# A linear-attention pair on one core: one key product is regrouped when it is saved, not when it is read

## The chip, the cores and the metric

The kernel runs on one core of one Trainium2 chip. The metric is the device time of one execution in microseconds (us). An execution that was profiled has, beside its time, a span: the stretch that the profile covers. The smallest difference that a measurement of this kernel tells from none is taken as 2%.

## The reference

Two linear-attention blocks, A and B, read the same input x (2048 rows of 640) with weights of their own, and a sigmoid gate mixes their outputs.

```python
qkv = (x @ wqkv)            # 640 -> 3 * 640, 32 heads of 20
phi = lambda t: jnp.where(t > 0, t + 1, jnp.exp(t)) + 1e-6
pq, pk = phi(q), phi(k)
kv  = einsum("bhsd,bhse->bhde", pk, v)
z   = einsum("bhsd->bhd", pk)
o   = einsum("bhqd,bhde->bhqe", pq, kv) / (einsum("bhqd,bhd->bhq", pq, z)[..., None] + 1e-6)
block(x) = o @ wo
g = sigmoid((x * gate_w).sum(-1))
out = g * block_A(x) + (1 - g) * block_B(x)
```

All tensors are bfloat16; sums are kept in float32.

## The kernel before, in words

The 2048 rows are 16 tiles of 128 rows. The work runs in stages whose order on TensorE (PE) is written out by hand in the string `MAIN`.

- **Keys.** For each tile and each block, five pairs of matmuls (lines 653 and 654, 512 and 128 or 129 columns, one pair for each 128 of the 640 inputs) make the keys of the tile in two PSUM banks. Column 640 of block B holds the gate sum of each row. `k_post` turns them into phi(k): ScalarE (ACT) reads PSUM and takes the exponential into `EK`, a part of `EKT` (line 699); VectorE (DVE) clamps it to at most 1 and adds 1e-6 (`kt`, line 702); then either ACT writes relu(k) into `PKS` (line 711 where both blocks of a tile take this way, line 726 otherwise) and DVE adds the two (`ka`, line 717 for both blocks, line 729 for one), or DVE does maximum and addition from PSUM in one instruction (`ks`, line 738). The list `KRS` says which tile and block takes which way. For block B, ACT also takes exp(-gate) into `GE` (line 690).
- **Regrouping.** The keys come out of the matmul with column d of 640 at place (m, g), g running fastest in steps of 5. `k_post` reads them as (g, m): `psg` is a view with a step of five float32 values in the inner loop.
- **Tiles 12 and 13.** `ks_unit(6)` makes the keys of these two tiles and both blocks by a scheme of seven half products in place of eight (tokens `K6.1` to `K6.7` in `MAIN`, line 809). Two half products are saved from PSUM to float32 buffers in SBUF, `s5` and `s2` (`save`, line 815, on ACT; the buffers `KQ` lie in `PQ0`, which the profile calls `PQ`). `comb` (line 820, DVE) later adds the other half: in step 3 PSUM plus `s2` back into PSUM, in step 7 PSUM plus `s5` into `s5`. So the keys of block B of tile 13 stand in SBUF and not in PSUM when `k_post` takes exponential, relu and gate from them. The weight sums for the scheme are four DVE instructions in `kw_sums` (line 767), the row sums five in `kx_sums` (line 787).
- **Sums over rows.** The tokens G0 to G4 multiply phi(k) with x (line 1156) in groups of eight matmuls, one for each pair of tiles. They too use the scheme of seven products: their factors are differences of phi(k) (`s_pair`, line 879) and of x (`t_all`, line 904), made on DVE. `G0.1`, `G3.1` and so on are the steps; a step numbered 1 or 2 leaves out the last pair of tiles, 14 and 15, which 8 and 9 add later.
- After this come the queries (lines 1035 and 1124), the small products with the value and output weights, the denominators (line 1410) and the output products (line 1546), which are stored by DMA.

**What sets the order.** PE follows the order in which the operations are created. ACT, DVE and the DMA queues get their order from a planner in the kernel (`Sched.run`) before anything is emitted: each operation has an estimated cost, PSUM banks are given to buffers when they are planned to be free, and for each engine the operation that can start first is taken, or, at equal start, the one created first. The planner takes an engine to be free again `LATE` nanoseconds before the end of the operation's cost:

```python
self.occ = max(40.0, cost - LATE.get(eng, 0.0))
LATE = {"ACT": 110.0, "DVE": 80.0}
def act_cost(n): return 190 + 0.833 * n
```

The cost doesn't depend on where an operation reads or with what step.

Of the kernel before, what the change touches and what calls it, by code (L numbers as in the profile page):

```python
# [6 lines left out]
ACT = mybir.ActivationFunctionType  # L7
ALU = mybir.AluOpType
# [3 lines left out]
D = 640  # L12
# [3 lines left out]
NC = 5  # L16
# [49 lines left out]
WPDVE = ("A1", "B0",)  # L66
QD = ("0.0A0", "0.0A1", "0.1B0", "0.1B1", "0.2A0", "0.2B0", "0.2B1", "0.3A0", "1.0B1",)
RD = ("A0", "A1", "A4", "B0",)
LATE = {"ACT": 110.0, "DVE": 80.0}


class Buf:
# [37 lines left out]
class Sched:  # L110
# [9 lines left out]
    def op(self, eng, fn, cost, ins=(), outs=(), after=(), prio=None, name="", dma=None):  # L120
        if eng == "ACT" and dma is None:
            after = list(after) + self.consts
        o = Op(eng, fn, cost, list(ins), list(outs), after, (self.base or len(self.ops)) if prio is None else prio, name, dma)
        self.ops.append(o)
        return o
# [184 lines left out]
def body(nc, A_x, A_wqkv, A_wo, B_x, B_wqkv, B_wo, gate_w, out, log=None):  # L310
# [25 lines left out]
    GE = sb("GE", [128, NT], f32)  # L336
# [40 lines left out]
    KQ = [PQ0f[:, 1296 * i : 1296 * i + 1296].bitcast(f32) for i in range(2)]  # L377
# [53 lines left out]
    op = sch.op  # L431

    def psw(b, w):
        if b.pool == "kq":
            return KQ[b.slot][:, 0:w]
        return PS[:, b.slot : b.slot + b.n, :].rearrange("p a b -> p (a b)")[:, 0:w]

    chain, loading = {}, [1]
# [18 lines left out]
    def act_cost(n):  # L457
        return 190 + 0.833 * n
# [209 lines left out]
    def k_post(t, units):  # L668

        n = len(units)  # L670
        ek, ek2 = Buf("ek", "ek", n, (0, 2, 4)), Buf("ek2")
        exps = []

        def ev(i):
            return EK[:, ek.slot + i, :]

        def evg(i):
            return ev(i).rearrange("p (g m) -> p g m", g=NC)

        def psg(ps):  # L680
            return psw(ps, D).rearrange("p (m g) -> p g m", g=NC)

        for i, (X, ps, relu) in enumerate(units):
            first = []
            if X == "B":
                b = Buf("ge")
                bge.append(b)
                op(
                    "ACT",
                    lambda e, ps=ps: e.activation(GE[:, t : t + 1], psw(ps, D + 1)[:, D : D + 1], ACT.Exp, scale=-1.0),  # L690
                    200.0,
                    ins=[ps],
                    outs=[b],
                    name="ge",
                )
                first = [b]
            b = Buf("ekx")
            exps.append(b)
            op("ACT", lambda e, i=i, ps=ps: e.activation(evg(i), psg(ps), ACT.Exp), act_cost(D), ins=[ps] + first, outs=[ek, b], name="ke")  # L699
        op(  # L700
            "DVE",
            lambda e: e.tensor_scalar(EK[:, ek.slot : ek.slot + n, :], EK[:, ek.slot : ek.slot + n, :], 1.0, EPS, op0=ALU.min, op1=ALU.add),  # L702
            dve4(n * D),
            ins=[ek],
            outs=[ek2],
            name="kt",
        )
        if n == 2 and units[0][2] and units[1][2]:
            rk = Buf("rk")
            for X, ps, relu in units:  # L710
                op("ACT", lambda e, X=X, ps=ps: e.activation(pkt(X, t), psg(ps), ACT.Relu), act_cost(D), ins=[ps], outs=[rk], name="kr")  # L711
            pk = Buf("pk%d" % t)
            bpk["A", t] = bpk["B", t] = pk

            def both(e):
                v = PKv[:, :, t % 2, t // 2, :]
                return e.tensor_tensor(out=v, in0=v, in1=EK[:, ek.slot : ek.slot + 2, :].rearrange("p x (g m) -> p (x g) m", g=NC), op=ALU.add)

            pk_last.append(op("DVE", both, dve2(2 * D), ins=[rk, ek, ek2], outs=[pk], name="ka"))
            pk_last.append(pk_last[-1])  # L720
            return
        for i, (X, ps, relu) in enumerate(units):
            pk = bpk[X, t] = Buf("pk%s%d" % (X, t))
            if relu:
                rk = Buf("rk")
                op("ACT", lambda e, X=X, ps=ps: e.activation(pkt(X, t), psg(ps), ACT.Relu), act_cost(D), ins=[ps], outs=[rk], name="kr")  # L726
                o = op(
                    "DVE",
                    lambda e, X=X, i=i: e.tensor_tensor(out=pkt(X, t), in0=pkt(X, t), in1=evg(i), op=ALU.add),
                    dve2(D),  # L730
                    ins=[rk, ek, ek2],
                    outs=[pk],
                    name="ka",
                )
            else:
                o = op(
                    "DVE",
                    lambda e, X=X, i=i, ps=ps: e.scalar_tensor_tensor(pkt(X, t), psg(ps), 0.0, evg(i), op0=ALU.max, op1=ALU.add),  # L738
                    dve1(D),
                    ins=[ps, ek, ek2],  # L740
                    outs=[pk],
                    name="ks",
                )
            pk_last.append(o)
# [29 lines left out]
    def kx_sums():  # L774
        t1, t2 = 256 * KU, 256 * KU + 128
        a11, a12, a21, a22 = [XT[:, c : c + 2, lo : lo + 128] for lo in (t1, t2) for c in (0, 2)]
        for k, in0, in1, need in (
# [13 lines left out]
                name="kx",  # L791
            )

    def ks_unit(j):
        px, py, pz = [Buf("k", "ps", 2, cover=(512, 129)) for _ in range(3)]
        py.need = (512, 128)
        s2, s5 = [Buf("kq", "kq") for _ in range(2)]
        d = {}
        t1, t2 = 2 * j, 2 * j + 1

        def xt(c, h):
            return XT[:, c, 256 * j + 128 * h : 256 * j + 128 * h + 128]

        def mm(ps, w, first, prs, ins, after=()):
            def fn(e):
                a = psw(ps, w)
                for i, (m, l) in enumerate(prs):
                    for lo, hi in ((0, 512), (512, w)):
                        r = e.matmul(a[:, lo:hi], l, m[:, lo:hi], start=(first and i == 0), stop=(i == len(prs) - 1), skip_group_check=not first)  # L809
                return r  # L810

            kpe[:] = [op("PE", fn, len(prs) * (mm_cost(512) + mm_cost(128)), ins=ins, outs=[ps], after=after, name="K%d" % j)]

        def save(dst, ps, w):
            return op("ACT", lambda e: e.activation(psw(dst, w), psw(ps, w), ACT.Copy), act_cost(w), ins=[ps], outs=[dst], name="ksv")

        def comb(ps, src, into_src):
            return op(
                "DVE",
                lambda e: e.tensor_tensor(out=psw(src if into_src else ps, D + 1), in0=psw(ps, D + 1), in1=psw(src, D + 1), op=ALU.add),  # L820
                dve1(D + 1),
                ins=[ps, src],
                outs=[src if into_src else ps],
                name="kcm",
            )

        bx = [bxt[t1], bxt[t2]]

        def step(n):
            if n == 1:  # L830
                mm(px, D + 1, True, [(WK["A"][:, c, :], xt(c, 0)) for c in range(2)], bx + [bwk["A", c] for c in range(2)] + [bwz])
                d[1] = op("ACT", lambda e: e.activation(psw(py, D), psw(px, D), ACT.Copy), act_cost(D), ins=[px], outs=[py], name="kfk")
            elif n == 2:
                mm(py, D, False, [(WK["A"][:, c, :], xt(c, 0)) for c in range(2, 5)], bx + [bwk["A", c] for c in range(2, 5)])
            elif n == 5:
                mm(pz, D + 1, True, [(KW[1][:, c, :], KX[1][:, c, :]) for c in range(2)] + [(WK["B"][:, 4, :], xt(4, 1))], bx + [bkw[1], bkx[1], bwk["B", 4], bgc])
                d[5] = save(s5, pz, D + 1)
            elif n == 6:
                mm(px, D + 1, False, [(KW[2][:, c, :], KX[2][:, c, :]) for c in range(2)], [bkw[2], bkx[2]], [d[1]])
                d[2] = save(s2, px, D + 1)  # L840
            elif n == 3:
                mm(pz, D + 1, False, [(WK["B"][:, 2 + c, :], KX[4][:, c, :]) for c in range(2)] + [(WK["B"][:, 4, :], KX[5])], [bkx[4], bkx[5], bgc] + [bwk["B", c] for c in range(2, 5)], [d[5]])
                comb(pz, s2, False)
                k_post(t1, [("A", py, "%dA" % t1 in KRS), ("B", pz, "%dB" % t1 in KRS)])
            elif n == 7:
                mm(px, D + 1, False, [(KW[3][:, c, :], KX[3][:, c, :]) for c in range(2)], [bkw[3], bkx[3]], [d[2]])
                d[7] = comb(px, s5, True)
            elif n == 4:
                mm(px, D, False, [(KW[4][:, c, :], xt(2 + c, 1)) for c in range(2)] + [(WK["A"][:, 4, :], xt(4, 1))], bx + [bkw[4], bwk["A", 4]], [d[7]])
                for X, ps in (("B", s5), ("A", px)):  # L850
                    k_post(t2, [(X, ps, "%d%s" % (t2, X) in KRS)])

        return step
# [874 lines left out]
```

## Time and profile before

| | |
|---|---|
| time, median of three runs | 176.8 us |
| the three runs | 176.8, 176.49, 1020.49 us |
| time of the profiled execution | 176.63 us |
| span of the profiled execution | 175.2 us |
| granted TensorE clock | 1.00 |
| PE busy | 172.1 us, 1331 matmuls |
| DVE busy | 140.3 us, 246 instructions |
| ACT busy | 116.2 us, 221 instructions |

The table is read from the head and part 1 of the profile. A row of a view gives the line of the kernel, the engine and operation, what is written and what is read, the shape, the count, and busy time with the mean of one. "PEld" is the weight load that goes ahead of each matmul. In the view in order of time, a row has start, duration and, in brackets, how long the engine stood idle before it and who ended that. Instructions of one engine overlap a little there: the next starts before the one before it has ended, so what one instruction takes of its engine is the distance to the next start.

### The profile page before, as it was taken

To read this page: it belongs to the slowest core of one execution; us is meant where nothing else is said; L and a number is where in the kernel's file an instruction comes from. 1 tells how busy PE (TensorE), PEld (TensorE's weight loads), DVE (VectorE), ACT (ScalarE), POOL (GpSimd) and SP (SyncE) were. 2 spreads that over 40 slices of the span, in tenths; PEclk is the share of its full clock that TensorE was granted. 3 is DMA by queue.
4 is the path that set the end of the run, shared out by engine and by line. 5 is a ranking of instruction groups with operands and counts; after the bars stand their busy time and mean duration, and the time that the engine had idled before them with its cause. 6 is when DMAs were issued, how large, how long until landed. Compare 5 with 4: busy or idle time off the path is not lost.

```text
span 175.2 us, 3364 instructions
## 1 busy us (share of the span) xinstructions
PE 172.1 (98%) x1331; PEld 107.6 (61%) x1331; DVE 140.3 (80%) x246; ACT 116.2 (66%) x221; POOL 4.9 (3%) x17
## 2 busy tenths in 40 slices
PE   9999999999999999999999999999999999999995
PEld 4555555555557776665666665655556667777773
DVE  2298996999989957668975798799999985999441
ACT  5377889998972232558695788848799874366132
POOL 2000000000000070000000000000000000000000
PEclk9999999999999999999999999999999999999999
DMA  6979999990000015310531703267671011451144
GB/s 191 315 127 126 236 354 365 357 190 4 4 0 0 0 37 101 74 38 0 136 99 37 224 4 75 49 168 210 226 186 40 0 41 28 96 185 41 37 147 153
DMA packets 33035, 20.59 MB, mean 118 GB/s; under 512 B 18260, under 2 KB 32892, under 8 KB 33020
## 3 DMA queue, kind: packets, MB, share of 16 engines
q1 hardware_dynamic: 32062, 19.76, 43.4%
q10 hardware_dynamic: 958, 0.63, 1.2%
q8 instruction: 10, 0.16, 0.4%
q14 instruction: 5, 0.04, 0.1%
HBM read 10.88 MB, written 4.26 MB: 86 GB/s over the span
## 4 chain that ended last, share of the span: by engine, by line
PE 94%; ACT 4%; issue 1%; DVE 0%; ACTq 0%
PE ps L1546 22%; PE ps L1156 20%; PE ps L653 16%; PE ps L1035 13%; PE ps L1124 10%; PE ps L654 4%; ACT EKT L699 3%; PE ps L809 3%; PE ps L580 1%; PE ps L1410 1%; PE ps L1336 1%; PE ps L1304 1%; ACT PKS L711 1%; PE ps L593 1%; ACT PKS L726 0%
## 5 line engine op out<-in xcount | busy, mean ns | idle before, releaser
L653 PE MATMUL ps<-WKW,XT 128*128 128x512 bf16 x140 | 39.5, 383 | 0.2 <-ACT GE L690 0.2
L654 PE MATMUL ps<-WKW,XT 128*128 128x128 bf16 (+1 forms) x140 | 30.9, 221 | 0.0
L699 ACT ACTIVATE EKT<-ps 128x640 bf16<-128x640 f32 x31 | 21.6, 711 | 5.3 <-PE ps L654 4.8
L653 PEld LDWEIGHTS ps<-WKW,XT 128*128 128x128 bf16 x140 | 13.8, 99 | 17.2 <-issue 0.7
L1156 PE MATMUL ps<-TX,PKS 128*128 128x321 bf16 (+1 forms) x160 | 24.1, 300 | 0.0
L1156 PEld LDWEIGHTS ps<-TX,PKS 128*128 128x128 bf16 x160 | 15.7, 98 | 7.4
L1156 PE MATMUL ps<-XN,PKS 128*128 128x321 bf16 (+1 forms) x120 | 18.7, 300 | 0.4 <-ACT PKS L711 0.3
L1156 PEld LDWEIGHTS ps<-XN,PKS 128*128 128x128 bf16 x120 | 11.5, 98 | 6.3 <-ACT PKS L711 1.1
L1184 ACT ACTIVATE EKT<-ps 128x321 f32<-128x321 f32 (+1 forms) x15 | 6.5, 438 | 11.1 <-PE ps L1156 8.9
L654 PEld LDWEIGHTS ps<-WKW,XT 128*128 128x128 bf16 x140 | 13.8, 99 | 0.0
L1065 ACT ACTIVATE EQ<-ps 128x512 bf16<-128x512 f32 x18 | 10.6, 599 | 3.8 <-DVE ps L1049 2.4
L879 DVE TENSOR_TENSOR PKS<-PKS 128x1280 bf16<-128x1280 bf16 (+2 forms) x20 | 12.8, 682 | 0.0
L702 DVE TENSOR_SCALAR EKT<-EKT 128x1280 bf16<-128x1280 bf16 (+1 forms) x19 | 8.3, 436 | 4.4 <-ACT EKT L699 4.2
L1189 DVE TENSOR_TENSOR WKW<-ps,EKT 128x320 bf16<-128x320 f32 x15 | 7.3, 486 | 5.2 <-PE ps L1156 5.0
L711 ACT ACTIVATE PKS<-ps 128x640 bf16<-128x640 f32 x16 | 11.4, 711 | 0.0
L1135 ACT ACTIVATE EQ<-ps 128x1024 bf16<-128x1024 f32 x8 | 8.2, 1029 | 4.4 <-PE ps L1124 3.4
L1035 PE MATMUL ps<-XT,WQA 128*128 128x512 bf16 x36 | 10.4, 379 | 0.0
L1124 PE MATMUL ps<-XT,WQA 128*128 128x512 bf16 x40 | 9.2, 381 | 0.0
L1124 PE MATMUL ps<-XT,WQB 128*128 128x512 bf16 x40 | 9.0, 381 | 0.0
L1611 ACT ACTIVATE PKS<-ps 128x320 bf16<-128x320 f32 x8 | 3.5, 437 | 8.1 <-PE ps L1546 8.1
L738 DVE SCALAR_TENSOR_TENSOR PKS<-ps,EKT 128x640 bf16<-128x640 f32 x10 | 8.2, 818 | 0.0
L1569 DVE TENSOR_TENSOR PKS<-ps,EKT 128x320 bf16<-128x320 f32 x9 | 4.4, 491 | 4.1 <-PE ps L1546 3.8
(179 smaller groups left out, 325.5 us busy)
## 6 DMA issues: line engine op xcount, KB each, us to landing
out_dram<-PKS SPq DMA_DIRECT2D x15, 160.0 KB, 1.8
XN<-in_A_x_dram SPq DMA_DIRECT2D x1, 2240.0 KB, 9.3
WKW<-in_A_wqkv_dram SPq DMA_DIRECT2D x5, 160.0 KB, 3.8
WKW<-in_B_wqkv_dram SPq DMA_DIRECT2D x5, 160.0 KB, 3.7
WQA<-in_A_wqkv_dram SPq DMA_DIRECT2D x1, 800.0 KB, 11.0
WQB<-in_B_wqkv_dram SPq DMA_DIRECT2D x1, 800.0 KB, 12.2
WVA<-in_A_wqkv_dram SPq DMA_DIRECT2D x1, 800.0 KB, 11.3
PKS<-in_B_wqkv_dram SPq DMA_DIRECT2D x1, 800.0 KB, 4.8
```

Of the source, the lines that this page charges most:

```text
L653: e.matmul(a[:, 0:512], l, WK[X][:, c, 0:512], start=(c == 0), stop=(c == NC - 1))
L654: return e.matmul(a[:, 512:w], l, WK[X][:, c, 512:w], start=(c == 0), stop=(c == NC - 1))
L699: op("ACT", lambda e, i=i, ps=ps: e.activation(evg(i), psg(ps), ACT.Exp), act_cost(D), ins=[ps] + first, outs=[ek, b], name="ke")
L702: lambda e: e.tensor_scalar(EK[:, ek.slot : ek.slot + n, :], EK[:, ek.slot : ek.slot + n, :], 1.0, EPS, op0=ALU.min, op1=ALU.add),
L711: op("ACT", lambda e, X=X, ps=ps: e.activation(pkt(X, t), psg(ps), ACT.Relu), act_cost(D), ins=[ps], outs=[rk], name="kr")
L738: lambda e, X=X, i=i, ps=ps: e.scalar_tensor_tensor(pkt(X, t), psg(ps), 0.0, evg(i), op0=ALU.max, op1=ALU.add),
L879: lambda e: e.tensor_tensor(out=out, in0=a, in1=b, op=ALU.subtract),
L1035: r = e.matmul(PS[:, ps.slot, :], w, x, start=(first and i == 0), stop=(i == len(prs) - 1), skip_group_check=not first)
L1065: o = [op("ACT", lambda e: e.activation(EQ[:, eq.slot + h, :], pv(), ACT.Exp), act_cost(512), ins=ins, outs=[eq], name="qe")]
L1124: r = e.matmul(PS[:, ps.slot + h, :], WQ[X][:, c, g::5], XT[:, c, 1024 + 512 * h : 1536 + 512 * h], start=(c == 0), stop=(c == NC - 1))
L1156: r = e.matmul(PS[:, ps.slot, 0:w], reg[:, j, :], mov(j, w), start=(first and j == 0), stop=(j == 7), skip_group_check=not first)
L1546: r = e.matmul(PS[:, ps.slot, 0:HALF], reg(g), mov(g), start=(first and g == 0), stop=(g == NC - 1), skip_group_check=not first)
```

## The change

Three things change.

1. `s5` is stored regrouped. `save` with `turn` true reads PSUM through `psx`, 645 columns as (m, g), 129 by 5, and writes `KQ` as (g, m), five rows of 129 values, through `kqg`. `comb` of step 7 reads PSUM through `psx` and adds into `kqg` in the same order. `s2` is stored as it was.
2. `k_post` reads `s5` without a step: `psg` gives, for a buffer of the pool `kq`, five runs of 128 neighbouring values; the gate column is value 128 of the first row of 129.
3. `LATE["ACT"]` goes from 110 to 125, so that the planner takes ACT to be free 15 ns sooner after each of its operations.

The change's own description adds that the sums of key weights come two tiles later. The diff holds no line that places `kw_sums`; the order of operations on ACT and DVE and the banks of PSUM come out of the planner anew, with the new constant.

```diff
-LATE = {"ACT": 110.0, "DVE": 80.0}
+LATE = {"ACT": 125.0, "DVE": 80.0}
...
     def psw(b, w):
-        if b.pool == "kq":
-            return KQ[b.slot][:, 0:w]
         return PS[:, b.slot : b.slot + b.n, :].rearrange("p a b -> p (a b)")[:, 0:w]
...
         def psg(ps):
+            if ps.pool == "kq":
+                return kqg(ps)[:, :, 0:128]
             return psw(ps, D).rearrange("p (m g) -> p g m", g=NC)
...
-                    lambda e, ps=ps: e.activation(GE[:, t : t + 1], psw(ps, D + 1)[:, D : D + 1], ACT.Exp, scale=-1.0),
+                    lambda e, ps=ps: e.activation(GE[:, t : t + 1], kqg(ps)[:, 0, 128:129] if ps.pool == "kq" else psw(ps, D + 1)[:, D : D + 1], ACT.Exp, scale=-1.0),
...
+    def kqg(b):
+        return KQ[b.slot][:, 0:645].rearrange("p (g m) -> p g m", g=NC)
+
+    def psx(b):
+        return psw(b, 645).rearrange("p (m g) -> p g m", g=NC)
...
-        def save(dst, ps, w):
-            return op("ACT", lambda e: e.activation(psw(dst, w), psw(ps, w), ACT.Copy), act_cost(w), ins=[ps], outs=[dst], name="ksv")
+        def save(dst, ps, turn):
+            return op("ACT", lambda e: e.activation(kqg(dst), psx(ps), ACT.Copy) if turn else e.activation(KQ[dst.slot][:, 0 : D + 1], psw(ps, D + 1), ACT.Copy), act_cost(D + 1), ins=[ps], outs=[dst], name="ksv")
...
-                lambda e: e.tensor_tensor(out=psw(src if into_src else ps, D + 1), in0=psw(ps, D + 1), in1=psw(src, D + 1), op=ALU.add),
+                lambda e: e.tensor_tensor(out=kqg(src), in0=psx(ps), in1=kqg(src), op=ALU.add)
+                if into_src
+                else e.tensor_tensor(out=psw(ps, D + 1), in0=psw(ps, D + 1), in1=KQ[src.slot][:, 0 : D + 1], op=ALU.add),
...
-                d[5] = save(s5, pz, D + 1)
+                d[5] = save(s5, pz, True)
...
-                d[2] = save(s2, px, D + 1)
+                d[2] = save(s2, px, False)
```

## The prediction

> **What bounds the kernel now.** I read the head of the page first, then the view of waits, then the view in order of time wherever PE waits for another engine.
>
> ```profile
> span 175.2 us, 3364 instructions
> PE 172.1 (98%) x1331; PEld 107.6 (61%) x1331; DVE 140.3 (80%) x246; ACT 116.2 (66%) x221; POOL 4.9 (3%) x17
> ```
>
> PE is busy for 172.1 of 175.2 us. An edit on ACT or DVE can therefore only win what PE stands still for, and it can lose much more than that. Where PE waits for ACT or DVE, the view of waits says:
>
> ```profile
> PEld ps L1156 <- ACT PKS L711: 1.1, 2, 0.7
> PE ps L653 <- ACT GE L690: 0.2, 1, 0.2
> ```
>
> The larger one, 1.1 us in two waits, is one place: the change from keys to sums over rows. In order of time, ACT and PE's weight loads there:
>
> ```profile
> 45.71 0.21 ACT L690 ACTIVATE GE<-PQ 128x1 f32<-128x1 f32 x1
> 45.81 1.40 ACT L726 ACTIVATE PKS<-PQ 128x640 bf16<-128x640 f32 x1
> 47.08 1.40 ACT L699 ACTIVATE EKT<-PQ 128x640 bf16<-128x640 f32 x1
> 48.34 1.33 ACT L699 ACTIVATE EKT<-ps 128x640 bf16<-128x640 f32 x2
> 49.50 0.22 ACT L690 ACTIVATE GE<-ps 128x1 f32<-128x1 f32 x1
> 49.55 0.77 ACT L711 ACTIVATE PKS<-ps 128x640 bf16<-128x640 f32 x1
> 50.14 0.78 ACT L699 ACTIVATE EKT<-ps 128x640 bf16<-128x640 f32 x1
> 50.72 0.79 ACT L711 ACTIVATE PKS<-ps 128x640 bf16<-128x640 f32 x1
> ...
> 49.18 0.51 PEld L1156 LDWEIGHTS ps<-XN,PKS 128*128 128x128 bf16 x4
> 50.37 0.80 PEld L1156 LDWEIGHTS ps<-XN,PKS 128*128 128x128 bf16 x7 [0.68 <-ACT PKS L711]
> 51.56 2.43 PEld L1156 LDWEIGHTS ps<-XN,PKS 128*128 128x128 bf16 x19 [0.39 <-ACT PKS L711]
> ```
>
> ACT has no gap from 45.71 to 51.5. PE stands until the relu of tile 15 block A (49.55) has freed its PSUM banks, so that G0.1 can start, and again until the relu of block B (50.72) has, for G3.1: 0.68 + 0.39 = 1.07 us. Ahead of both, in the same queue, are the two reads of `s5` out of SBUF (EKT<-PQ and PKS<-PQ), each with 1.40 us twice as long as its neighbours. They are what the change touches.
>
> **The change part by part.** *The two reads of s5.*
>
> ```profile
> L726 ACT ACTIVATE PKS<-PQ 128x640 bf16<-128x640 f32 x1 | 1.4, 1398 | 0.0
> L699 ACT ACTIVATE EKT<-PQ 128x640 bf16<-128x640 f32 x1 | 1.4, 1397 | 0.0
> L1065 ACT ACTIVATE EQ<-ps 128x512 bf16<-128x512 f32 x18 | 10.6, 599 | 3.8 <-DVE ps L1049 2.4 <-PE ps L1035 1.2
> L1065 ACT ACTIVATE EQ<-PKS 128x512 bf16<-128x512 f32 x6 | 3.8, 629 | 2.5 <-DVE PKS L1049 2.4
> ```
>
> The last two rows are the same exponential from PSUM and from a float32 buffer in SBUF without a step: 599 and 629 ns, so SBUF as such costs 30 ns. The same reads with a step of five from PSUM take 711 ns (row L699 EKT<-ps below), and 1397 with that step from SBUF. What costs is the step in SBUF, and the change removes it: I take 711 + 30 = 740 ns each. The nearest row without a step from SBUF, scaled by 128 more values at the slope between 640 and 512 from PSUM ((711 - 599) / 128 = 0.875 ns), gives 629 + 112 = 741. Bounds: 711 (no cost of SBUF at all) and 1397 (the runs of 128 with a jump bring nothing). ACT's queue moves by the distance of starts: now 47.08 - 45.81 = 1.27 and 48.34 - 47.08 = 1.26; afterwards about 0.6, like the neighbours (50.72 - 50.14 = 0.58, and 30 ns more). Together 2.53 - 1.22 = 1.31 us. The gate read stays one value.
>
> *The save and the sum of s5*, now with the step on the PSUM side and 645 columns for 641:
>
> ```profile
> L699 ACT ACTIVATE EKT<-ps 128x640 bf16<-128x640 f32 x31 | 21.6, 711 | 5.3 <-PE ps L654 4.8
> L832 ACT ACTIVATE ps<-ps 128x640 f32<-128x640 f32 x1 | 0.7, 699 | 0.0
> L815 ACT ACTIVATE PQ<-ps 128x641 f32<-128x641 f32 x2 | 1.3, 735 | 0.0
> L738 DVE SCALAR_TENSOR_TENSOR PKS<-ps,EKT 128x640 bf16<-128x640 f32 x10 | 8.2, 818 | 0.0
> L820 DVE TENSOR_TENSOR PQ<-ps,PQ 128x641 f32<-128x641 f32 x1 | 0.8, 820 | 0.0
> ```
>
> On ACT a step of five in PSUM costs 711 against 699 without (L832), on DVE 818 (L738, with the step) against 820 (L820, without). So save and sum cost what they did, 735 and 820 ns, and 4 columns more (4 x 0.875 = 4 ns). Bounds: nothing, or, if they paid what SBUF pays for the step, 1397 - 711 = 0.69 us each.
>
> [...]
>
> *What PE gets.* The last key matmul of tile 15:
>
> ```profile
> 47.76 0.22 PE L654 MATMUL ps<-WKW,XT 128*128 128x129 bf16 x1
> ```
>
> 1.31 us off ACT's queue before 48.34 brings the relu at 49.55 to 48.24 and the one at 50.72 to 49.41, unless PE makes them wait: that matmul ends at 47.98, so the gate read and what follows can go from about 48.1. The relu of block A then ends at 49.0, PE needs its banks at 49.69; that of block B ends at 50.2, PE needs them at 49.69 + 7 x 0.138 = 50.66. Both waits go: 1.07 us.
>
> *Is anything late next?* DVE must keep up with PE, which comes 1.07 us sooner.
>
> ```profile
> 49.10 0.33 DVE L702 TENSOR_SCALAR EKT<-EKT 128x640 bf16<-128x640 bf16 x1 [0.22 <-ACT EKT L699]
> 50.94 0.49 DVE L702 TENSOR_SCALAR EKT<-EKT 128x1280 bf16<-128x1280 bf16 x1 [0.38 <-ACT EKT L699]
> 52.09 0.82 DVE L717 TENSOR_TENSOR PKS<-PKS,EKT 128x1280 bf16<-128x1280 bf16 x1
> 56.84 2.49 DVE L879 TENSOR_TENSOR PKS<-PKS 128x256 bf16<-128x256 bf16 x6
> ...
> 51.56 17.77 PE ps L1156 x129
> ...
> 56.88 2.35 PE L1156 MATMUL ps<-TX,PKS 128*128 128x321 bf16 x16
> ```
>
> DVE waits for ACT twice here, 0.22 + 0.38 = 0.60 us; that goes, so DVE comes 0.60 sooner, 0.47 less than PE. Two deadlines follow. G0.9 needs the keys of tile 15, ready at 52.09 + 0.82 = 52.91; it is matmul 17 after 51.56, at 51.56 + 16 x 0.138 = 53.77 (17.77 / 129 = 0.138): slack 0.86. G0.6 needs the second difference, the first 256-wide one (281 ns) at 56.84, ready at 57.12, for its seventh matmul at 56.88 + 6 x 0.138 = 57.71: slack 0.59. Both exceed 0.47, the second by 0.12 only. Without that cover each 0.1 of DVE delay is 0.1 of time.
>
> *The constant.* Distances of ACT's starts on the chip are 0.58 to 0.60 us for 640 elements; the planner's 723 - 110 = 613 becomes 598 ns. So the new order is planned on figures nearer to the chip, but it is a new order, and PE's hand-written one stays. The weight sums now:
>
> ```profile
> 9.17 0.82 DVE L767 TENSOR_TENSOR GSA<-WKW 128x1282 bf16<-128x1282 bf16 x1
> 11.61 0.82 DVE L767 TENSOR_TENSOR GSB<-WKW 128x1282 bf16<-128x1282 bf16 x1
> 12.35 0.82 DVE L738 SCALAR_TENSOR_TENSOR PKS<-ps,EKT 128x640 bf16<-128x640 f32 x1
> 17.30 0.49 DVE L702 TENSOR_SCALAR EKT<-EKT 128x1280 bf16<-128x1280 bf16 x1 [0.77 <-ACT EKT L699]
> 25.01 0.49 DVE L702 TENSOR_SCALAR EKT<-EKT 128x1280 bf16<-128x1280 bf16 x1 [0.35 <-ACT EKT L699]
> 28.19 0.49 DVE L702 TENSOR_SCALAR EKT<-EKT 128x1280 bf16<-128x1280 bf16 x1 [1.42 <-ACT EKT L699]
> 36.11 0.71 PE L809 MATMUL ps<-GSA,PQ 128*128 128x512 bf16 x4
> ```
>
> The first and the third of the four are shown; all lie ahead of the wait at 17.30, and they are needed first at 36.11. Reading the planner's rule, the first has no rival for its place, while the third is ahead of the key step at 12.35 by a near tie that 15 ns can turn. Two sums moved behind take 2 x 0.74 (12.35 - 11.61) = 1.48 us of DVE later; its waits for ACT that follow hold 0.77 + 0.35 + 1.42 = 2.54. So the delay is absorbed before it reaches G0.6. In front, the steps they made wait free PSUM up to 0.74 sooner, which may take the 0.2 us wait of line 653, which lies among the first tiles. Bounds: -0.2 and, if nothing is absorbed, the rival below. I take 0.
>
> **Sum**, on the profiled execution: 176.63 - 1.07 = 175.56, say 175.6. This execution has 1.43 us beside its span and lies 0.17 below the median of 176.8.
>
> **The rivals.** *Half comes back on DVE.* The new order puts other work ahead of DVE's two waits, and DVE comes no sooner. Then G0.9 wants tile 15 at 53.77 - 1.07 = 52.70 and gets it at 52.91 (0.21 lost), and G0.6 wants its difference at 57.71 - 0.86 = 56.85 and gets it at 57.12 (0.27). Of 1.07 remain 0.59: 176.0. For it speaks the thin cover of 0.12, against it that both waits name ACT's exponentials, which come sooner.
>
> *The moved sums overrun DVE: slower.* All four sums go into the keys' stretch, where DVE is nearly full:
>
> ```profile
> 20.00:33.00 13.00, 13.00 (x97) 7.40 (x96) 11.12 (x23) 11.72 (x23) 0.00 (x0) 1.00 1.07 338
> 33.00:46.00 13.00, 13.00 (x98) 7.39 (x96) 12.68 (x17) 12.14 (x25) 0.00 (x0) 1.00 0.49 122
> ```
>
> Behind the bounds and the length of a stretch stand the busy times of PE, PEld, DVE and ACT: DVE has 11.12 and 12.68 of 13 us. If the gaps cannot be used, because they are waits for ACT that recur elsewhere, 4 x 0.74 = 2.96 us arrive at the difference that G0.6 waits for. It is then ready at 57.12 + 2.96 - 0.60 = 59.48 against 57.71 now: 1.8 us slower than before, 178.4. It decides from 1.19 us of overrun (0.59 + 0.60): above, the kernel is slower than before, whatever ACT wins. With half of the gaps of 2.54 used, 1.7 us arrive: 0.5 slower, 177.1, which I take as its price. Against it: the need at 36.11 is far and the gaps are real.
>
> *It does not do what it says.* Runs of 128 from SBUF cost as much as the step: 176.6. The 629 ns of line 1065 speak against it.
>
> *The step in PSUM costs.* 0.69 us on ACT at the save lies seven us ahead of the queue that matters; 0.69 on DVE at the sum eats the 0.60 it gains, which is the first rival's case: 176.0. Rows L699 and L738 speak against both. [...]
>
> **How the numbers follow.** Chances: the forecast 0.60 (its own range 175.2 to 175.9: the 0.2 us wait of line 653 gained below, 0.3 of DVE delay above), half given back on DVE 0.18, the overrun or another such collision of the new order 0.17, no effect 0.03, the PSUM step 0.02. The range must reach to 176.0 and to most of the overrun's case: 175.1 to 177.5. Faster by over 2% (below 173.3) would need more standing time than PE has with ACT or DVE, 1.3 us: 0.02. Slower by over 2% (above 180.3) needs a collision beyond the worst priced here: 0.05. Within 2%: 0.93. 2% is about what a measurement of this kernel can tell from no change, so the forecast's 0.6% should come out as no difference by that bound.
>
> **What would show it.** In the new profile L726 PKS<-PQ and L699 EKT<-PQ take 711 to 760 ns; L815 stays near 735 and L820 near 820; the wait PEld L1156 <- ACT L711 is gone or under 0.2 us; DVE's waits of 0.22 and 0.38 are gone; PE's busy time stays 172.1 and the span falls to about 174.1. The forecast is wrong if those reads stay at 1.4 us, if PE waits for L717 or L879 between 50 and 60 us, or if PE waits anywhere it does not now.

## The result, and the profile after

The changed kernel takes 175.95 us in the median, the kernel before 176.9 in the same set of runs; the ratio is 0.9955, with a 95% interval of 0.9936 to 0.9974. By the ratio that is 0.8 us (0.5 to 1.1) less: a small but clear gain, and no difference by the bound of 2%. One run of the kernel before, of 1020.49 us, is left out of the ratio, which compares mean times; the medians lie 0.95 us apart. The profiled execution took 175.72 us, with a span of 174.3.

The head of the page after:

```profile
span 174.3 us, 3365 instructions
PE 171.6 (98%) x1331; PEld 107.7 (62%) x1331; DVE 140.1 (80%) x246; ACT 115.0 (66%) x221; POOL 4.9 (3%) x17
```

The groups of instructions that read or write the saved half product (`PQ`):

```profile
L726 ACT ACTIVATE PKS<-PQ 128x640 bf16<-128x640 f32 x1 | 0.7, 747 | 0.0
L699 ACT ACTIVATE EKT<-PQ 128x640 bf16<-128x640 f32 x1 | 0.7, 745 | 0.0
L821 ACT ACTIVATE PQ<-ps 128x645 f32<-128x645 f32 x1 | 0.7, 731 | 0.0
L826 DVE TENSOR_TENSOR PQ<-ps,PQ 128x645 f32<-128x645 f32 x1 | 0.8, 824 | 0.0
```

The two reads fell from 1397 and 1398 to 745 and 747 ns. The save (line 821, 815 before) and the sum (826, 820 before), which now read PSUM with the step, cost what they did: 731 and 824 ns, 735 and 820 before.

The same stretch in order of time, ACT and PE after (products on x are now line 1164):

```profile
45.66 0.75 ACT L726 ACTIVATE PKS<-PQ 128x640 bf16<-128x640 f32 x1
46.28 0.74 ACT L699 ACTIVATE EKT<-PQ 128x640 bf16<-128x640 f32 x1
...
48.13 0.74 ACT L711 ACTIVATE PKS<-ps 128x640 bf16<-128x640 f32 x1
...
49.30 0.76 ACT L711 ACTIVATE PKS<-ps 128x640 bf16<-128x640 f32 x1
...
47.67 8.47 PE L1164 MATMUL ps<-XN,PKS 128*128 128x321 bf16 x61
55.98 2.35 PE L1164 MATMUL ps<-TX,PKS 128*128 128x321 bf16 x16
```

The 61 products on XN run without a break. Before, they were in two parts, and the first product on TX came at 56.88, as the prediction shows:

```profile
47.82 2.21 PE L1156 MATMUL ps<-XN,PKS 128*128 128x321 bf16 x15
50.37 6.67 PE L1156 MATMUL ps<-XN,PKS 128*128 128x321 bf16 x46 [0.34 <-ACT PKS L711]
```

From the first product on XN to the first on TX PE took 56.88 - 47.82 = 9.06 us before and 55.98 - 47.67 = 8.31 after: 0.75 us less. This stretch, with the same 61 matmuls in every kernel here, is the measure for the experiments below. The load of the first weights lies ahead of it; PE's wait for them differs from one execution to the next (for `in_A_wqkv` 0.41 us at 4.85 before, 0.53 at 4.91 after). The other 0.15 us were there when the stretch began (47.82 and 47.67). Of these, 0.09 come from the wait of line 653 among the first tiles. PE in order of time, before and then after (line 651):

```profile
12.35 0.38 PE L653 MATMUL ps<-WKW,XT 128*128 128x512 bf16 x1
12.99 0.38 PE L653 MATMUL ps<-WKW,XT 128*128 128x512 bf16 x1 [0.21 <-ACT GE L690]
...
12.29 0.38 PE L651 MATMUL ps<-WKW,XT 128*128 128x512 bf16 x1
12.84 0.38 PE L651 MATMUL ps<-WKW,XT 128*128 128x512 bf16 x1
```

From start to start these took 0.64 us before and 0.55 after, where the pairs ahead of them start 0.27 us apart. So PE still stands here, for 0.28 us in place of 0.37. The view of PE's waits no longer lists it; after, it has one row:

```profile
PE ps L578 <- DVE ONE L476: 0.3, 1, 0.3
```

That is the wait at the very start. PE is 0.90 us ahead at the first product on TX (56.88 and 55.98), and the span is 0.9 us shorter: behind the stretch nothing more was won or lost.

### The profile page after: what moved, and what is told of

Same layout as the page of the kernel before. It is cut to its first block, busy times and chain, and to the rows that moved or that the text cites. A ratio compares the mean times of both kernels' runs of the same rounds, so it can differ in the third digit from the quotient of the medians.

```text
span 174.3 us, 3365 instructions
## 1 busy us (share of the span) xinstructions
PE 171.6 (98%) x1331; PEld 107.7 (62%) x1331; DVE 140.1 (80%) x246; ACT 115.0 (66%) x221; POOL 4.9 (3%) x17
## 4 chain that ended last, share of the span: by engine, by line
PE 96%; DMA 2%; SPq 0%; ACT 0%; issue 0%
PE ps L1164 22%; PE ps L1554 22%; PE ps L651 17%; PE ps L1043 13%; PE ps L1132 10%; PE ps L652 4%; PE ps L815 3%; DMA WKW<-in_A_wqkv_dram 2%; PE ps L1418 1%; PE ps L1344 1%; PE ps L1312 1%; SPq L444 0%; ACT PKS L1619 0%; PE ps L628 0%
```

## The experiments

**Layout alone.** The new layout, the old constant. With it the planner's order on every engine, and the banks, are those of the kernel before.

```diff
-LATE = {"ACT": 125.0, "DVE": 80.0}
+LATE = {"ACT": 110.0, "DVE": 80.0}
```

> Only the layout of s5 changes; the constant stays at 110, so every engine keeps the order of before. Theory (the two reads of s5 hold ACT's queue, ACT holds the PSUM banks, PE stands for them): both reads take 745 ns in place of 1397, the two waits of PE's weight loads (0.68 and 0.39 us) go, and PE's stream is 0.75 us ahead of before from 52 us on, with the 0.1 us of the wait at 12.96 not won: time 0.75 us under the kernel before, 176.15. Rival (the gain comes from the new order that the constant makes): PE's stream shifts by under 0.2 us, time as before, 176.9.

Measured: 176.08 us, ratio 0.9964 (0.9950 to 0.9977), 0.64 us less than before. PE in order of time:

```profile
48.03 8.47 PE L1164 MATMUL ps<-XN,PKS 128*128 128x321 bf16 x61
56.34 2.35 PE L1164 MATMUL ps<-TX,PKS 128*128 128x321 bf16 x16
```

A row of the view of its waits:

```profile
PE ps L651 <- ACT GE L690: 0.2, 1, 0.2
```

56.34 - 48.03 = 8.31 us: the whole 0.75 of the stretch comes from the layout, in the old order. The 0.2 us wait among the first tiles stays, as expected: 0.64 us from start to start, as before. (This execution came to the stretch 0.36 us later than the changed kernel did: 0.09 of that is this wait, and the rest was there ahead of it.) The expectation's 745 ns and 0.75 us are figures of the changed kernel's profile; what it put to the test is that the layout alone gives them.

**The constant alone.** The old layout, `LATE["ACT"]` at 125; the order is that of the changed kernel.

```diff
-LATE = {"ACT": 110.0, "DVE": 80.0}
+LATE = {"ACT": 125.0, "DVE": 80.0}
```

> Only the constant changes; s5 keeps its layout, and the order is that of the changed kernel. Theory: the reads of s5 stay at 1.40 us, the two waits for ACT near 50 us stay at 1.0 to 1.1 us in the weight loads, only the wait for the gate read at 12.96 goes: PE's stream 0.1 us ahead, time 176.8. Rival (the order makes the gain): the waits near 50 us go although the reads stay long, stream 0.8 us ahead, 176.05.

Measured: 176.6 us, ratio 0.9989 (0.9978 to 1.0000): 0.2 us less, with an interval that ends at no change. The group of one of the two reads:

```profile
L699 ACT ACTIVATE EKT<-PQ 128x640 bf16<-128x640 f32 x1 | 1.4, 1412 | 0.0
```

PE in order of time, with two of its weight loads:

```profile
47.70 2.21 PE L1156 MATMUL ps<-XN,PKS 128*128 128x321 bf16 x15
50.26 0.80 PEld L1156 LDWEIGHTS ps<-XN,PKS 128*128 128x128 bf16 x7 [0.68 <-ACT PKS L711]
51.44 2.57 PEld L1156 LDWEIGHTS ps<-XN,PKS 128*128 128x128 bf16 x20 [0.38 <-ACT PKS L711]
56.76 2.35 PE L1156 MATMUL ps<-TX,PKS 128*128 128x321 bf16 x16
```

56.76 - 47.70 = 9.06, exactly as before: the new order does nothing for the stretch. The wait of line 653 among the first tiles is shorter here, 0.55 us from start to start as in the changed kernel. So the order is worth some 0.1 us of PE's stream, and the layout the rest: the rival that the order makes the gain falls.

What the constant does can be seen on DVE after 11 us in this kernel:

```profile
11.30 0.69 DVE L702 TENSOR_SCALAR EKT<-EKT 128x640 bf16<-128x640 bf16 x2
11.91 1.55 DVE L738 SCALAR_TENSOR_TENSOR PKS<-ps,EKT 128x640 bf16<-128x640 f32 x2
13.38 0.82 DVE L767 TENSOR_TENSOR GSB<-WKW 128x1282 bf16<-128x1282 bf16 x1
```

The third weight sum (GSB<-WKW) starts at 13.38 in place of 11.61, behind the key steps (`ks`) of block B of tiles 0 and 1, which free PSUM; no line of the program moves it. This is the later place of the sums that the change's description names. That these earlier key steps are what shortens the wait of line 653 fits the order, but no view shows which read freed the banks that PE took there.

**How much of ACT's time PE needs.** Relus of `s5` are added to the changed kernel behind the exponential of `s5`, one or two; the planner gives them no time, so that the order stays.

```diff
+for k in range(EXTRA if ps.pool == "kq" else 0):
+    x = op("ACT", lambda e, k=k, ps=ps: e.activation(PQ0f[:, 3744 + D * k : 4384 + D * k].rearrange("p (g m) -> p g m", g=NC), psg(ps), ACT.Relu), 0.0, ins=[ps], name="spare")
+    x.occ = 0.0
```

One:

> The changed kernel with one more relu of s5 (640 values, into a part of PQ0 that is free then) in ACT's queue just behind the exponential of s5; the order of everything else is that of the changed kernel. It gives back half of what ACT won, 0.62 us. Theory: the relu of tile 15 block A then ends at 49.5 and PE asks for its banks at 49.58, the one of block B ends at 50.7 and PE asks at 50.54; PE loses 0 to 0.1 us, time 175.95 to 176.05. Rival (each us on ACT is a us of time here, ACT is the chain): 0.62 us more, 176.57.

Measured: 175.91 us, ratio 0.9956 (0.9939 to 0.9973), the same as the changed kernel. PE in order of time, with a weight load:

```profile
47.69 8.55 PE L1168 MATMUL ps<-XN,PKS 128*128 128x321 bf16 x61
50.76 3.25 PEld L1168 LDWEIGHTS ps<-XN,PKS 128*128 128x128 bf16 x25 [0.23 <-ACT PKS L712]
56.08 2.35 PE L1168 MATMUL ps<-TX,PKS 128*128 128x321 bf16 x16
```

The stretch is 8.39: 0.62 us more on ACT cost PE 0.08. The weight loads show one gap of 0.23.

Two:

> The same with two more relus, 1.25 us, about all that ACT won. Theory: both waits come back as in the kernel before, 1.0 us in the gaps of the weight loads and 0.65 to 0.75 us in PE's stream, time 176.6 to 176.7. Rival (one for one): 1.25 us more, 177.2. If the gaps of the weight loads are the loss, as the forecast took them: 1.0 us more, 176.95.

Measured, PE in order of time:

```profile
48.73 2.21 PE L1168 MATMUL ps<-XN,PKS 128*128 128x321 bf16 x15
57.74 2.35 PE L1168 MATMUL ps<-TX,PKS 128*128 128x321 bf16 x16
```

The waits of its weight loads:

```profile
PEld ps L1168 <- ACT PKS L712: 1.0, 2, 0.6
```

The stretch is 57.74 - 48.73 = 9.01: with ACT's time given back, 0.70 of the 0.75 is lost again, and both waits stand where they stood. The time went to 176.89 us, ratio 1.0008 (0.9994 to 1.0022), which is 0.2 above what theory expected, and by itself fits a loss of 1.0 us as well; the stretch is what rejects that. Its profiled execution lost more than usual to the first weights (a wait of 0.84 us for `in_B_wqkv`, at 8.71), so spans are not compared here. Whether that is why the median lies 0.2 higher was not settled.

**DVE's cover.** The same with one more instruction on DVE behind the key step of tile 13 block A, first a plain sum, then a slower instruction on the same operands.

```diff
+v = PQ0f[:, 3744:5024].rearrange("p (a b) -> p a b", a=2)
+x = op("DVE", lambda e: e.tensor_tensor(out=v, in0=XN[:, 0:2, 0:D], in1=XN[:, 2:4, 0:D], op=ALU.add), 0.0, ins=bxn[0:4], after=[pk_last[-1]], name="spare")
+x.occ = 0.0
```

The slower one is a `scalar_tensor_tensor` with maximum and addition in its place.

> The changed kernel with one more sum on DVE (1280 bfloat16 from XN into a free part of PQ0, 0.74 us of DVE) behind the key step of tile 13 block A; the order of everything else is that of the changed kernel. Theory (DVE has cover: tile 15's keys are there at 51.98 and PE asks for them at 52.85, the difference for G0.6 at 55.92 and PE asks at 56.80): no loss, the stretch from the first product on XN to the first on TX stays at 8.31 us, time 175.95. Rival (DVE is the next bound, with the 0.12 us of cover that the forecast counted): 0.6 us more, 176.55.

> The same with a slower DVE instruction on the same operands (maximum, then sum). If it takes 1.4 us of DVE, tile 15's keys come 1.4 - 0.82 = 0.58 us late: the stretch grows to 8.9 us, time 176.5. Rival (cover of 0.12 us): 1.3 us more, 177.2. If it takes 0.74 us like the plain sum, as in that run.

The plain sum: 176.13 us, ratio 0.9951 (0.9934 to 0.9969), stretch 56.18 - 47.87 = 8.31, no loss. PE in order of time:

```profile
47.87 8.47 PE L1167 MATMUL ps<-XN,PKS 128*128 128x321 bf16 x61
56.18 2.35 PE L1167 MATMUL ps<-TX,PKS 128*128 128x321 bf16 x16
```

The slow one: 176.51 us, ratio 0.9972 (0.9956 to 0.9988), stretch 56.87 - 47.96 = 8.91, as expected. DVE and PE in order of time:

```profile
50.73 1.48 DVE L861 SCALAR_TENSOR_TENSOR PQ<-XN 128x1280 bf16<-128x1280 bf16 x1
52.86 0.82 DVE L717 TENSOR_TENSOR PKS<-PKS,EKT 128x1280 bf16<-128x1280 bf16 x1
...
47.96 5.35 PE L1167 MATMUL ps<-XN,PKS 128*128 128x321 bf16 x38
53.73 2.97 PEld L1167 LDWEIGHTS ps<-XN,PKS 128*128 128x128 bf16 x23 [0.76 <-DVE PKS L717]
56.87 2.35 PE L1167 MATMUL ps<-TX,PKS 128*128 128x321 bf16 x16
```

PE waits for the keys of tile 15 (line 717). Counted from the first product on XN, DVE came to them 1.41 us later than in the changed kernel (52.86 - 47.96 against 51.16 - 47.67), and PE lost 0.60: at this point DVE has 0.8 us of cover in the changed kernel. And here, too, the gap in the weight loads (0.76) is larger than what PE lost (0.60).

**The price of a step by itself.**

> None of the block's work is in it: single instructions of 640 values, one behind the other, that read float32 and bfloat16 from SBUF and float32 from PSUM with steps of 1 to 16 elements, and ACT writes with steps of 2, 5 and 8; the output is filled with zeros. [...] Rival (any step in SBUF costs): 1.4 us from step 2 on in both types. If DVE pays like ACT, its sum with a stepped float32 operand in SBUF goes from 820 to 1400 ns or more at a step of 5; if not, 820 at all steps.

Each reads 640 values, in one execution. In the view in order of time, ACT from float32 in SBUF (`SF`) at steps of 1, 2, 3, 4 and 5; from bfloat16 (`SH`) at 4, 5 and 8; writing bfloat16 (`AW`) at steps of 2, 5 and 8; DVE with one float32 operand in SBUF at 2 and 5:

```profile
6.79 0.74 ACT L335 ACTIVATE AF<-SF 128x640 bf16<-128x640 f32 x1
7.56 0.77 ACT L335 ACTIVATE AF<-SF 128x640 bf16<-128x640 f32 x1
8.36 1.05 ACT L335 ACTIVATE AF<-SF 128x640 bf16<-128x640 f32 x1
9.44 1.33 ACT L335 ACTIVATE AF<-SF 128x640 bf16<-128x640 f32 x1
10.80 1.34 ACT L335 ACTIVATE AF<-SF 128x640 bf16<-128x640 f32 x1
...
21.94 0.77 ACT L335 ACTIVATE AH<-SH 128x640 bf16<-128x640 bf16 x1
22.74 0.91 ACT L335 ACTIVATE AH<-SH 128x640 bf16<-128x640 bf16 x1
23.67 1.33 ACT L335 ACTIVATE AH<-SH 128x640 bf16<-128x640 bf16 x1
...
30.14 0.91 ACT L335 ACTIVATE AW<-SF 128x640 bf16<-128x640 f32 x1
31.09 1.98 ACT L335 ACTIVATE AW<-SF 128x640 bf16<-128x640 f32 x1
33.09 3.03 ACT L335 ACTIVATE AW<-SF 128x640 bf16<-128x640 f32 x1
...
37.01 0.82 DVE L349 TENSOR_TENSOR DF<-ps,SF 128x640 f32<-128x640 f32 x1
39.18 1.28 DVE L349 TENSOR_TENSOR DF<-ps,SF 128x640 f32<-128x640 f32 x1
```

The groups of instructions with the step in PSUM, ACT at 1, 2, 3, 5 and 6 and DVE at 2, 5 and 6:

```profile
L335 ACT ACTIVATE AP<-ps 128x640 bf16<-128x640 f32 x5 | 3.5, 703 | 0.2
L349 DVE TENSOR_TENSOR DP<-ps,SF 128x640 f32<-128x640 f32 x3 | 2.5, 824 | 0.1
```

From SBUF, 8 bytes from value to value (2 float32, 4 bfloat16) cost 0.77 us, 10 bytes 0.91, 12 bytes 1.05, 16 bytes 1.33 and 20 bytes 1.34: the price rises up to 16 bytes and no further at 20. At 8 and at 16 bytes it is the same for both types. In between it rises evenly, by 0.14 us for each 2 bytes. The rival, that any step costs its full price, falls: 8 bytes cost 0.03 us more than none. From PSUM the step is free here: ACT takes 703 ns in the mean of steps 1 to 6, DVE 824 ns at 2, 5 and 6, against 699 (line 832) and 820 (line 820) without a step in the kernel before. DVE's 1.28 us at a step of 5 in SBUF lies between the two expectations, 1.4 and 0.82: it pays for the step, 0.46 us against ACT's 0.60. The step of 5 cost ACT 1.40 us in the kernel and 1.34 here; that 0.06 is not explained.

## Why the prediction was right, point by point

The measured 175.95 us lies in the stated range of 175.1 to 177.5, but just above the forecast case's own 175.2 to 175.9, and beside 176.0, the price of two of the rivals. What speaks for the forecast's mechanism is therefore the trace and the experiments, not the time.

- *The two reads of s5*: 740 ns forecast, 745 and 747 measured; ACT's queue came 1.27 us sooner at the first relu of the pair (49.55 - 48.13 = 1.42, of which 0.15 were there before), where 1.31 were forecast. Right.
- *Save and sum*: 735 and 820 forecast, 731 and 824 measured. Right.
- *What PE gets*: both waits went, as forecast, by the layout alone. The size was wrong: 1.07 us forecast, 0.75 measured. This is the term that failed. The forecast added the gaps of the weight loads, 0.68 + 0.39. But weight loads run ahead of the matmuls: after, the load for the first product on TX starts 0.14 us ahead of it (55.98):

```profile
55.84 2.15 PEld L1164 LDWEIGHTS ps<-TX,PKS 128*128 128x128 bf16 x16
```

  After a gap, load and matmul start together (both at 50.37 before), and then the loads catch up: the seven loads at 50.37 took 0.80 us, where seven at the pitch of the matmuls (8.31 / 61 = 0.136, and 0.10 for one load) take 6 x 0.136 + 0.10 = 0.92. The experiments show the size: two gaps of 1.02 us in all for 0.70 lost with two more relus, one of 0.76 for 0.60 with the slow sum, one of 0.23 for 0.08 with one relu. With the 1.07 for 0.75 of the kernel before, each gap overstates the loss by 0.15 to 0.16 us. The right sum could be had from the profile before: there the 16 products on TX at 56.88 are followed by the next product at 59.06, 0.136 us for each; 61 matmuls of 0.136 us are 8.3 us, and PE took 9.06. PE's own gap in the view, 0.34, errs on the other side: the profile counts PE as busy for 8.66 of the 9.06 us before and for all of the 8.31 after, so 0.35 of the 0.75 counts as busy. The sign that PE's busy time stays at 172.1 us missed too: it fell to 171.6 (172.0 with the layout alone).
- *The constant*: taken as 0, with a bound of -0.2. It gave about 0.1: the third weight sum went behind the key steps, as named, and the wait of line 653 became 0.09 us shorter. It did not vanish, and that the one brought the other is not shown. DVE absorbed the moved sums, as forecast.
- *What is late next*: DVE was forecast to come 0.60 sooner and to have 0.12 us of cover at G0.6. It came sooner than that, 51.16 against 52.09 at tile 15's keys: 0.93, of which 0.15 were there before, so 0.78, as much as PE's 0.75. The forecast had added the gaps in brackets, 0.22 + 0.38; by the distances of starts, DVE stood for 0.29 and 0.45 us at these two places. The cover is 0.8 us at tile 15's keys, and 0.88 at G0.6 (55.92 against 56.80, the times in the expectation of the plain sum). Tile 15's keys after:

```profile
51.16 0.82 DVE L717 TENSOR_TENSOR PKS<-PKS,EKT 128x1280 bf16<-128x1280 bf16 x1
```

  The first rival, half given back on DVE, had no ground in this kernel; the slow sum shows that its mechanism is real and where it begins.
- *The sum*: 175.6 forecast, 175.95 measured. The forecast stood on a profiled execution, and between profiled executions the change won 0.91 us (176.63 and 175.72) where 1.07 were forecast: 0.32 too much for the two waits, less the 0.1 of the constant and some 0.06 that this execution was ahead when the first tiles began. The other 0.23 of the 0.39 (175.95 less 175.56) is base: the changed kernel's profiled execution lies that far below its median of 175.95.

No kernel here is faster than the changed one by more than the spread of its runs. PE no longer waits for ACT or DVE in this stretch, so more time off either would win nothing there.

## What to carry to other kernels

What the layout of a buffer costs is paid at each read, here 0.65 us at each of two (1397 and 1398 ns with the step, 745 and 747 without): turn the data where the turn is free (here the read out of PSUM, 731 ns for the save against 735) and let the later reads from SBUF run over neighbouring values. Judge a stall by the pace of the bound engine, count times the pitch of its instructions against the time it took, and not by the gap of a queue that runs ahead of it. Where an order comes from a planner that prices all reads alike, a slow read that it does not know of shows up as a wait elsewhere, behind the instructions that follow it in the queue (here 0.68 and 0.39 us of PE's weight loads behind the relus of tile 15).

## What the runs showed of the hardware that was not expected

- A step on the write side costs ACT far more than on the read side: 640 bfloat16 written to SBUF take 0.91 us at a step of 2, 1.98 at 5 and 3.03 at 8, against 0.74 without, where reads of bfloat16 at the same steps take 0.74, 0.91 and 1.33. A save that regroups by stepping its write, with float32 values, was not run; these prices suggest that it would cost ACT more than the step in the read out of PSUM, which was free.
- DVE pays for a step in SBUF too, 1.28 us at 5 float32 against 0.82 at 2, and not for one in PSUM (824 ns at 2, 5 and 6).
- ACT's price of a step in SBUF goes up gradually between 8 and 16 bytes, 0.77, 0.91 and 1.05 us at 8, 10 and 12 bytes, and is 1.33 to 1.34 at 16 and 20.
